# Row loads for the next sequence's statistics, asked for one unit earlier in the SP queue

## Chip, cores and metric

The kernel runs on one core of a Trainium2 chip. The metric is device time in microseconds (us) of one execution; the time of a kernel is the median of its timed runs. Beside them there is one execution under the hardware profiler, which has its own time and its own span (first to last instruction).

## What is computed

Routed attention over 4 sequences of 768 positions with 8 heads of 64, and then a block with layer norm and two weight matrices on the joined heads (512 wide, 2048 hidden):

```python
mask = q_assign[:, :, :, None] == k_assign[:, :, None, :]      # nearest of 16 centroids, q and k
scores = np.where(mask, scale * np.matmul(q, k.transpose(0, 1, 3, 2)), -1e9)
attn = softmax(scores)
x = np.matmul(attn, v)                                          # (B,H,S,D) -> (B,S,H*D)
...
mu = np.mean(x, axis=-1, keepdims=True)
var = np.mean((x - mu) ** 2, axis=-1, keepdims=True)
xn = (x - mu) / np.sqrt(var + 1e-06) * g_ln
ch = np.maximum(xn @ w_ch1, 0.0) @ w_ch2
return (x + ch).astype(np.float32)
```

The part that matters here is `mu` and `var` of each row of `x`, 768 rows for each sequence.

## The kernel before

**Stages.** The attention of all four sequences comes first (to about 318 us of the span). Its result `x` goes to DRAM twice: with the channels on the partitions (`xT_d`), and by rows (`x_d`: for each sequence six tiles of 128 rows by 512 columns). Then each sequence b = 0 to 3 passes the two weight layers: b = 0 from about 318 to 465 us, b = 1 to 603, b = 2 to 740, b = 3 to the end. While sequence b is in its first layer, the statistics of sequence b + 1 are made.

**Units.** The first layer of a sequence is cut into `NFH` = 8 units j = 0 to 7. For b = 1 a unit is `first_units(b, j)`: seven block products of a Strassen-Winograd scheme (`first_layer` with parts 1, 2, 4, 6, 3, 5, 7), each four matmul records of 128x384. A product goes to one of six PSUM banks (`ps_m`), and ScalarE (ACT) or VectorE (DVE) takes it out: `kept` (L878) is a copy by ACT, `add_relu` (L883) an addition by DVE, L891 the relu by ACT. For b = 2 a unit has smaller inner products besides (L1271); sequence 3 goes through `last_layer` and has no next sequence. The second layer of b = 1 to 3 is `deep_layer` (L1148).

**The statistics.** `rows_load(b, t)` (L557-561) asks for row tile t of sequence b: one DMA of 256 KB from `x_d[b][t]` into a buffer `xr`, of which there are two for b > 0. `norm_rows(b, t)` (L563-578) first calls `rows_load` for a later tile, and then, for b = 2 and 3, has ACT make the sum, the mean and the sum of squares of tile t (L572 to L574). So a buffer comes free when ACT has read the tile for the second time, at L574. `norm_stats`, at the end of unit 5, needs all six tiles.

Where the calls stand, for the tiles of sequence b + 1 in the first layer of b = 1 or 2:

- tiles 0 and 1 are asked for ahead of unit 0 (L1778-1779)
- tile 0 is worked on at the end of unit 0 (`unit_end(b, 0)`, L1740), and tile j in unit j = 1 to 5, after its product part 1 (L1628). At that point ACT stands between the copy `p` of part 1 (L878) and the relu of part 4 (L920)
- tile j + 1 is asked for by that same `norm_rows(b + 1, j)`, so it has the rest of unit j and the beginning of unit j + 1 to land

**The queues.** From the second sequence on (the block opened at L1731) the instructions of PE, DVE, ACT and SP stand in the order in which the Python code calls them. Nearly all DMAs of this stage are issued by SP, one after another; an issue that waits for a semaphore holds up those behind it.

**What else SP issues in b = 1.** `unit_end(1, j)` calls in this order: `leave(4)` (stores of turned rows, `x_d<-col`, L1221), `columns_load` (a load of 384 KB for the next turn, L534, for odd j), the four DVE operations of `w2_split` (L1065), pending jobs, ring loads for j > 4, the statistics' last steps, `leave` again, then `split()` (a store of 1 MB, `w_d<-wt`, L1066), and, for j = 1, 3, 4, `w2_back` (a load of 1 MB, `w_t`, L1044, which a split two units later reads).

**In b = 2** `unit_end` calls `leave(8)`: up to eight stores of finished output (`out_dram<-y`, L1221). `first_units` stores sums of w1 for the last sequence (L1311, L1320, L1322, L1330 into `w1_d`).

**The last sequence's loads.** `last_load(n, g)` (L1350-1359) brings such sums back. With n = 3 it issues two DMAs, into a buffer `a3` taken from the six of `unit` (192 KB) and into one of the two `xr` buffers (256 KB). The first of them, `last_load(3, 0)`, stands at L1784, right after the `deep_layer` of b = 2, which ends with products (3, 4) and (3, 3) and with `leave(len(leaving))` (L1596).

Of the kernel before, what the change touches and what calls it, by code (L numbers as in the profile page):

```python
# [23 lines left out]
def kernel(  # L24
# [12 lines left out]
    B, H, S, D = q.shape  # L37
# [519 lines left out]
    def rows_load(b, t):  # L557
        if t < NT and (b, t) not in rows:
            x = (ffn if b else last).tile([P, DM], F32, tag="xr", name="xr", bufs=2 + (not b))
            nc.sync.dma_start(out=x, in_=x_d[b][t])  # L560
            rows[b, t] = x

    def norm_rows(b, t):  # L563
        rows_load(b, t + 1 + (not b))
        x = rows.pop((b, t))
        if t == 0:
            moments[b] = small.tile([P, NT, 3], F32, tag="mv", name="mv")
        mv = moments[b]
        if b != 1:

            total, mean = mv[:, t, 0:1], mv[:, t, 1:2]
            nc.scalar.activation(x, x, AF.Identity, accum_out=total)  # L572
            nc.scalar.mul(mean, total, -1.0 / DM)
            nc.scalar.activation(x, x, AF.Square, bias=mean, accum_out=mv[:, t, 2:3])  # L574
            return
        bn = small.tile([P, 6], F32, tag="bn", name="bn")
        nc.vector.bn_stats(out=bn, in_=x)
        nc.vector.bn_aggr(out=mv[:, t, :2], in_=bn)
# [640 lines left out]
    def leave(n, queues=(nc.sync,)):  # L1219
        for i, (to, y) in enumerate(leaving[:n]):  # L1220
            queues[i % len(queues)].dma_start(out=to, in_=y)  # L1221
        del leaving[:n]
# [127 lines left out]
    def last_load(n, g):  # L1350
        if g >= NPU:
            return
        if n == 3:
            if "a3" not in last_w:
                last_w["a3"] = flat(unit("a3"))
            nc.sync.dma_start(out=last_w["a3"][:, : 3 * P], in_=w1_d[3][g][:, : 3 * P])
            nc.sync.dma_start(out=last_w[3], in_=w1_d[3][g][:, 3 * P :])
        else:
            nc.sync.dma_start(out=last_w[n][:, : w1_d[n].shape[2]], in_=w1_d[n][g])
# [102 lines left out]
    def deep_layer(b, more, st):  # L1462
# [64 lines left out]
        def onto(i, j):  # L1527
            return lambda: sum_onto(i, j)

        jobs = {  # L1530
            (4, 1): [lambda: first_layer(b, NFH - 1, 4) if more else outer_sums(NFH - 2, True)],
            (4, 2): [between],
            (4, 5): [lambda: rest_load(b, 0)],
            (4, 3): [rest(1, 0, 4)],
            (7, 6): [s4(0)], (7, 4): [s4(1)], (7, 3): [s4(2)], (1, 6): [s4(3)],
            (1, 4): [onto(4, 7)], (6, 3): [onto(6, 1)],
            (5, 4): [onto(4, 6)], (5, 3): [onto(5, 6)], (2, 6): [onto(7, 5)],
        }
# [3 lines left out]
        if more:  # L1542
            for at, (i, c) in (
                ((4, 4), (0, 0)), ((7, 5), (0, 1)), ((1, 3), (0, 2)), ((6, 6), (0, 3)),
                ((6, 5), (1, 0)), ((6, 4), (1, 1)), ((5, 6), (1, 2)), ((5, 5), (1, 3)),
            ):
                jobs.setdefault(at, []).append(norm(i, c))
            for at, c in (((4, 7), 1), ((7, 2), 2), ((7, 3), 3)):
                jobs.setdefault(at, []).append(lambda c=c: norm_load(b + 1, c))
            jobs[2, 4] = [out_of(1, 0, 4)]  # L1550
            jobs[2, 3] = [rest(0, 0, 2), lambda: rest_load(b, 1)]
            jobs[3, 6] = [lambda: x_sum(b + 1, 1), lambda: x_sum(b + 1, 2)]
            if b + 1 < LAST:
                jobs[3, 5] = [lambda: w1_sums(b + 1, 0, (0, 1))]
            else:
                jobs[2, 5].append(last_room)
                jobs.setdefault((2, 7), []).append(lambda: last_load(5, 0))
                jobs[2, 4].append(lambda: last_load(0, 0))
                jobs[3, 5] = [lambda: last_load(2, 0)]
            jobs[3, 7] = [lambda: first_layer(b + 1, 0, 1)]  # L1560
            later(
                *[None] * (b + 1 >= PAIRED), rest(1, 1, 7), out_of(1, 1, 7), out_of(0, 0, 2), None, *[None] * (b + 1 >= PAIRED),
                rest(0, 1, 3), out_of(0, 1, 3), None,
            )
        else:
            jobs[7, 2] = [lambda: rest_load(b, 1)]
            jobs[1, 3] = [rest(1, 1, 7)]
            jobs[5, 6] = [rest(0, 0, 1), onto(4, 6)]
            del jobs[5, 4]
            jobs[2, 5].append(rest(0, 1, 5))  # L1570
            jobs[2, 1] = [out_of(1, 0, 4)]
            jobs[2, 7].append(out_of(1, 1, 7))
            jobs[2, 3] = [out_of(0, 0, 2)]
# [91 lines left out]
    with tc.manual_schedule(engines={mybir.EngineType.PE, mybir.EngineType.DVE}):  # L1665
# [25 lines left out]
        def do(f, *args):  # L1691
# [4 lines left out]
        jobs = {  # L1696
            (1, 0): [
                do(first_layer, 0, NFH - 1, 4), do(first_layer, 0, NFH - 1, 3), do(relu, 1),
                do(hidden_sums, 1, range(3)),
            ],  # L1700
            (1, 1): [do(hidden_sums, 1, range(3, NFH - 1))],
            (1, 2): [do(hidden_sums, 1, range(NFH - 1, NFH)), do(w2_sum, st, 2), keep(2, 2)],
            (2, 0): [do(hidden_sums, 2, range(3))],
            (2, 1): [do(hidden_sums, 2, range(3, NFH))],
# [26 lines left out]
    with tc.manual_schedule(engines=order | {mybir.EngineType.SP}):  # L1731
        first.close()
        splits = first.enter_context(tc.tile_pool(name="splits", bufs=1))
        outer = {}

        def unit_end(b, j):

            if b + 1 < B:
                if j == 0:
                    norm_rows(b + 1, j)  # L1740
            if b == 1:
                leave(4)
                if asked and j % 2:
                    columns_load(row)
                if j == 0:
                    outer["ends"] = all_in_range()
                if j == 2:
                    outer["flag"] = flag_of(outer.pop("ends"))
                m = (1, 5, 3, 4, 2, 7, 6, None)[j]
                if m in SUMS:  # L1750
                    split = w2_split(m, outer.pop(("t", SUMS.index(m) + 1)))
                elif m:
                    split = w2_split(m, by_half(w2_block(*{1: (0, 0), 2: (1, 0), 3: (1, 1)}[m])))
                if j in (5, 6):
                    outer_late("s", "e", (0, 0), j - 5)
            while pending:
                job = pending.pop(0)
                if job is None:
                    break
                job()  # L1760
            if j > 4:
                for _ in range(4):
                    if ring["next"] < len(STEPS) * (b - 1) + RING:
                        ring_load(b)
            if b + 1 < B and j + 3 == NFH:
                norm_stats(b + 1)
            if b + 1 < B and j + 2 == NFH:
                norm_stat_rows(b + 1)
            leave(8 if b >= PAIRED else 4)
            if b == 1 and m:  # L1770
                split()
                if j in (1, 3, 4):
                    w2_back({1: 4, 3: 3, 4: 2}[j])

        for b in range(1, B):
            deep[b] = {}
            if b + 1 < B:
                rows_load(b + 1, 0)  # L1778
                rows_load(b + 1, 1)
            if b == 1:  # L1780
                w2_back(1)
                first_units(b, 0)
            elif b == LAST:
                last_load(3, 0)  # L1784
                last_layer(b)
            else:
                first_layer(b, 0, 6)
                w1_sums(b, 0, (2, 3))
                x_sum(b, 3)
                first_layer(b, 0, 5)  # L1790
                x_sum(b, 4)
                first_layer(b, 0, 7)
                w1_sums(b, 1)
                deep_room(b)
                outer_keep(b, 0)
                outer_keep(b, 1)
                pair_begin(b, 0)
            if b < LAST:
                unit_end(b, 0)
                for j in range(1, NFH):  # L1800
                    first_units(b, j)
                    unit_end(b, j)
                relu(len(summed))
            if b == LAST:
                pass
            elif b >= PAIRED:
                inner_sums(deep[b], ORDER[0], cs=slice(0, NQH - 1))
            else:
                inner_sums(deep[b], ORDER[0], cs=slice(NQH - 1, NQH))
            if b == 1:  # L1810
                first.close()
                units = pool("units", 1)
            deep_layer(b, b + 1 < B, deep[b])
        flag = outer["flag"]

# [230 lines left out]
```

## Time and profile before

| what | before |
|---|---|
| timed runs, us | 879.55, 880.76, 884.12 (median 880.76) |
| profiled execution, us | 884.5 |
| its span, us | 882.7 |
| busy in the span: PE, DVE, ACT | 98%, 83%, 46% |
| mean granted TensorE clock | 0.996 |
| first layer of b = 1, span us | 465 to 538 |
| first layer of b = 2, span us | 603 to 674 |

The page of a profile shows busy time by engine and by slice, the chain of work that ended last (followed back from the end), and groups of instructions with the idle time before them. PE is TensorE, PEld its weight loads, SPq SyncE issuing a DMA. A DMA issue is shown with the time at which it was issued; "us to landing" is the time from there until its data was there. The profiled execution is 3.7 us longer than the median of the timed runs; of that, 1.8 us lie outside its span.

### The profile page before, as it was taken

Reading aid. Unit: us, or ns where it says so; the run is one execution under the profiler, and the core shown is the slowest. Engines: PE = TensorE matmul, PEld = TensorE weight load, DVE = VectorE, ACT = ScalarE, POOL = GpSimd, SP = SyncE. Lnnn points to the kernel's source line nnn. Section 1 sums busy time; section 2 is a strip of 40 time slices with the busy share of each in tenths; the row PEclk is TensorE's granted clock in tenths of the full one; section 3 lists DMA queues with packets and bytes.
Section 4 is the critical chain, followed back from the end, with each engine's and each line's share of the span. In section 5 each row is a group of like instructions: output and inputs, shape, how many; then the busy total and the mean of one; then the engine's idle time right before and its main releaser. Section 6 shows DMA issues by size and latency. Waiting matters only on the chain.

```text
span 882.7 us, 13640 instructions
## 1 busy us (share of the span) xinstructions
PE 869.2 (98%) x4744; PEld 587.3 (67%) x4744; DVE 730.3 (83%) x1262; ACT 407.4 (46%) x758; POOL 77.6 (9%) x143
## 2 busy tenths in 40 slices
PE   8999999999999999999999899999999999999996
PEld 5444444444444445568886557997667998778996
DVE  6899999999999888959677677897877897767875
ACT  6777788888888823330004442102553111443110
POOL 1012121222222212110000000000000000000000
PEclk9999999999999999999999999999999999999999
DMA  7777889999986338876685789865567965564875
GB/s 160 138 128 128 150 172 189 194 217 190 185 193 181 98 108 210 235 193 218 182 196 165 228 257 307 275 193 144 130 185 247 294 202 148 128 185 124 275 196 112
DMA packets 258493, 164.68 MB, mean 187 GB/s; under 512 B 192992, under 2 KB 211440, under 8 KB 257392
## 3 DMA queue, kind: packets, MB, share of 16 engines
q1 hardware_dynamic: 227392, 144.43, 60.9%
q0 software_dynamic: 7776, 15.03, 8.8%
q10 hardware_dynamic: 23248, 4.25, 2.7%
q8 instruction: 40, 0.66, 0.3%
q14 instruction: 37, 0.30, 0.1%
HBM read 115.21 MB, written 40.07 MB: 176 GB/s over the span
## 4 chain that ended last, share of the span: by engine, by line
PE 93%; DMA 3%; DVE 1%; ACT 1%; SPq 1%; issue 0%; ACTq 0%; DVEq 0%
PE s_ps L401 17%; PE x_ps L852 17%; PE a_ps L413 14%; PE x_ps L1148 12%; PE z_ps L1148 6%; PE z_ps L852 6%; PE x_ps L961 5%; PE y_ps L1148 3%; PE z_ps L961 2%; PE x_ps L1271 2%; PE y_ps L852 2%; DMA xr<-x_d 2%; PE den_ps L469 1%; PE sim_ps L320 1%; PE y_ps L961 1%; PE z_ps L1271 1%
## 5 line engine op out<-in xcount | busy, mean ns | idle before, releaser
L401 PE MATMUL s_ps<-t,t 64*128 64x384 f32 x768 | 154.8, 483 | 0.0
L401 PEld LDWEIGHTS s_ps<-t,t 64*128 64x128 f32 x768 | 68.0, 187 | 39.0 <-issue 38.3
L1148 PE MATMUL x_ps<-lower,w 128*128 128x192 f32 x448 | 80.8, 326 | 0.5 <-DVE u L1163 0.5
L1148 PEld LDWEIGHTS x_ps<-lower,w 128*128 128x128 f32 x448 | 74.1, 190 | 1.6 <-DVE u L1163 0.7
L396 ACT ACTIVATE e<-s_ps 128x768 f32<-128x768 f32 x84 | 67.1, 812 | 6.9 <-PE s_ps L401 6.4
L396 ACT ACTIVATE w<-s_ps 128x768 f32<-128x768 f32 x80 | 64.5, 813 | 8.3 <-PE s_ps L401 7.7
L401 PE MATMUL s_ps<-mask,mask 64*128 64x384 bf16 x384 | 62.8, 323 | 1.0 <-ACT e L396 0.6
L891 ACT ACTIVATE lower<-lower 128x384 f32<-128x384 f32 x88 | 43.8, 520 | 42.2 <-DVE lower L883 28.7
L878 ACT COPY u<-x_ps 128x384 f32<-128x384 f32 x64 | 30.6, 478 | 62.1 <-PE x_ps L852 61.8
L413 PE MATMUL a_ps<-e,v_sb 128*64 128x384 f32 x336 | 57.6, 488 | 0.0
L878 ACT COPY p<-x_ps 128x384 f32<-128x384 f32 x32 | 15.3, 477 | 91.1 <-PE x_ps L852 85.9
L413 PE MATMUL a_ps<-w,v_sb 128*64 128x384 f32 x320 | 55.2, 488 | 0.0
L852 PE MATMUL x_ps<-xn,ws 128*128 128x384 f32 x128 | 48.1, 499 | 2.4 <-ACT u L878 2.4
L852 PE MATMUL x_ps<-xn,w 128*128 128x384 f32 x128 | 47.1, 491 | 0.0
L883 DVE TENSOR_TENSOR lower<-z_ps,u 128x384 f32<-128x384 f32 x40 | 22.2, 555 | 29.6 <-PE z_ps L852 20.3
L852 PE MATMUL x_ps<-xt,ws 128*128 128x384 f32 x128 | 46.6, 487 | 0.0
L852 PE MATMUL x_ps<-xt,w 128*128 128x384 f32 x128 | 46.5, 486 | 0.0
L413 PEld LDWEIGHTS a_ps<-e,v_sb 128*64 128x64 f32 x336 | 23.5, 137 | 31.8 <-issue 28.7
L1503 POOL DMA_DIRECT2D out_dram<-y_end x2 | 1.2, 598 | 487.2 <-DMA out_dram<-y 487.2
L413 PEld LDWEIGHTS a_ps<-w,v_sb 128*64 128x64 f32 x320 | 22.4, 137 | 30.4 <-issue 27.5
L401 PEld LDWEIGHTS <-mask 64*128 64x128 bf16 x384 | 19.0, 94 | 35.0 <-issue 10.0
L366 ACT ACTIVATE mask<-oh,far 32x384 bf16<-32x384 bf16 x61 | 37.3, 612 | 3.3 <-DVE oh L349 1.9
(296 smaller groups left out, 1807.8 us busy)
## 6 DMA issues: line engine op xcount, KB each, us to landing
w<-w_d SPq DMA_DIRECT2D x84, 256.0 KB, 3.2
raw<-in_moe_w_ch_dram SPq DMA_DIRECT2D x32, 512.0 KB, 4.9
w<-w_t SPq DMA_DIRECT2D x36, 256.0 KB, 4.6
w<-tb POOLq DMA_DIRECT2D x32, 256.0 KB, 5.6
w_d<-wt SPq DMA_DIRECT2D x7, 1024.0 KB, 5.4
w<-w_all SPq DMA_DIRECT2D x27, 256.0 KB, 3.1
v_sb<-in_v_dram SPq DMA_DIRECT2D x32, 192.0 KB, 4.5
xr<-x_d SPq DMA_DIRECT2D x24, 256.0 KB, 3.2
```

Source lines behind the costliest of these rows:

```text
L320: nc.tensor.matmul(sim[r : r + Q, :HC], cT[:, pr, :, :].rearrange("p j c -> p (j c)"), prepared[n][side][:, g * HC : (g + 1) * HC], start= ...
L366: nc.scalar.activation(out, oh[src, :], AF.Identity, bias=add, scale=factor)
L396: nc.scalar.activation(e, s[:, :, :HC], AF.Exp, scale=SCALE)
L401: nc.tensor.matmul(s[:, j, :HC], of_keys[:, keys], of_queries[:, o : o + HC], start=part == first, stop=part != first, skip_group_check=True,)
L413: nc.tensor.matmul(acc[j * D : (j + 1) * D, :HC], loaded[n]["v"][:, j, c, :], e[:, j, :], start=(c == 0), stop=(c == NT - 1),)
L852: nc.tensor.matmul(bank[:, :HC], lhs[:, c, :], rhs[:, c], start=first and c == 0, stop=c == NDH - 1, skip_group_check=True,)
L878: nc.scalar.copy(t, bank[:, :HC])
L883: nc.vector.tensor_tensor(h, bank[:, :HC], other, ALU.add)
L891: nc.scalar.activation(h, h, AF.Relu)
L961: nc.tensor.matmul(bank[:, :MH].rearrange("p (h f) -> p h f", h=2), hidden[lhs + (c,)][:, tt * P : (tt + 1) * P], rhs[:, :, c], start=firs ...
L1148: nc.tensor.matmul(bank, w[:, c, :], a[:, c], start=way in (1, 2, 5) and c == 0, stop=c == NQH - 1, skip_group_check=True,)
L1271: nc.tensor.matmul(bank, p["w"][way], p["x"][way], start=way in (1, 2, 5), stop=True, skip_group_check=True)
```

## The change

The load of row tile j + 2 is now called at the end of unit j (for j = 0 after `leave`, ahead of `split()`; for j > 0 at the very beginning of `unit_end`), for sequences 2 and 3. `norm_rows` asks for a later tile only for sequences 0 and 1, where the tile asked for is the same as before (t + 2 for 0, t + 1 for 1). `last_load(3, 0)` moves from the beginning of sequence 3 to a job after product (3, 4) of the `deep_layer` of b = 2. No arithmetic changes, and no buffer is added.

```diff
     def norm_rows(b, t):
-        rows_load(b, t + 1 + (not b))
+        if b < 2:
+            rows_load(b, t + 2 - b)
         x = rows.pop((b, t))
...
                 jobs[3, 5] = [lambda: last_load(2, 0)]
+                jobs.setdefault((3, 4), []).append(lambda: last_load(3, 0))
             jobs[3, 7] = [lambda: first_layer(b + 1, 0, 1)]
...
             if b + 1 < B:
                 if j == 0:
                     norm_rows(b + 1, j)
+                else:
+                    rows_load(b + 1, j + 2)
             if b == 1:
                 leave(4)
...
             leave(8 if b >= PAIRED else 4)
+            if j == 0 and b + 1 < B:
+                rows_load(b + 1, 2)
             if b == 1 and m:
                 split()
...
             elif b == LAST:
-                last_load(3, 0)
                 last_layer(b)
```

## The prediction, made before the changed kernel ran

> **What bounds the kernel now.** I read the page first (busy times, then the chain that ended last), then the chain in order of time for the first layer of b = 1, then the instructions of PE, ACT and SP there in order of time.
>
> ```profile
> PE   8999999999999999999999899999999999999996
> PE 93%; DMA 3%; DVE 1%; ACT 1%; SPq 1%; issue 0%; ACTq 0%; DVEq 0%
> ```
>
> PE is on the chain for 93% of the span and busy in nearly every slice. So a change of transfers can gain only where PE stands still; one slice in the middle is not full. The 3% of DMA on the chain are the place to look. In order of time:
>
> ```profile
> 478.26 5.05 DMA xr<-x_d
> ...
> 486.18 10.28 DMA xr<-x_d
> ...
> 499.08 0.38 ACT u L878
> 499.46 0.04 issue
> 499.50 4.54 PE x_ps L852 x8
> 504.04 1.29 PE y_ps L852 x4
> ```
>
> The columns are start, duration and what. Two row tiles of the next sequence are on the chain; the second takes 10.28 us to land and leads over ACT to a PE product. PE's own list around it:
>
> ```profile
> 494.36 1.45 PE L852 MATMUL z_ps<-xn,ws 128*128 128x384 f32 x4
> 495.65 1.45 PE L852 MATMUL z_ps<-xt,ws 128*128 128x384 f32 x4
> 499.50 2.80 PE L852 MATMUL x_ps<-xn,ws 128*128 128x384 f32 x4 [2.40 <-ACT u L878]
> 502.10 1.95 PE L852 MATMUL x_ps<-xn,w 128*128 128x384 f32 x4
> 503.88 1.45 PE L852 MATMUL y_ps<-xn,w 128*128 128x384 f32 x4
> ```
>
> One product starts 1.29 us after the one before it (495.65 - 494.36). Here the third starts 3.85 us after the second, and it and the next are slow besides. ACT, at the same time:
>
> ```profile
> 490.69 0.48 ACT L878 COPY p<-x_ps 128x384 f32<-128x384 f32 x1 [0.92 <-PE x_ps L852]
> 496.49 0.63 ACT L572 ACTIVATE xr<-xr 128x512 f32<-128x512 f32 x1 [5.32 <-DMA xr<-x_d]
> ```
>
> ACT waits 5.32 us for row tile 3 (unit 3), and the relus and bank copies queued behind it wait too. PE used up the free banks during the first 2.9 us of that and then stood. SP shows why the tile was late:
>
> ```profile
> 478.26 0.50 SPq L560 DMA_DIRECT2D xr<-x_d  x1
> 479.20 4.29 SPq L1221 DMA_DIRECT2D x_d<-col  x4
> 483.53 0.55 SPq L534 DMA_DIRECT2D col<-xT_d  x1
> 485.15 0.38 SPq L1066 DMA_DIRECT2D w_d<-wt  x1
> 485.58 0.51 SPq L1044 DMA_DIRECT2D w_t<-w_t  x1
> 486.18 0.38 SPq L560 DMA_DIRECT2D xr<-x_d  x1
> 493.28 0.37 SPq L1066 DMA_DIRECT2D w_d<-wt  x1
> 493.74 0.46 SPq L560 DMA_DIRECT2D xr<-x_d  x1
> ```
>
> The request stands behind the four small-grained stores, a load of 384 KB, a store of 1 MB and a load of 1 MB. From 483 to 492 us the view by stage gives a DMA share of 1.02 and 283 GB/s: the engines are full.
>
> **What the Trainium skill says.** "DMA: Bandwidth & Descriptors", section "Queues, rings and completion order", has the descriptors of one issuing engine consumed in ring order on the shared DMA engines. The trace agrees: 256 KB takes 10.28 us behind 2 MB, but 3.2 us in the median over all row tiles. Its "Rules for kernel authors" advise issuing a DMA early and waiting late, which is the form of this change. "TensorE: Matmul & The Clock Gate", section "What's actually happening", says that an idle PE falls to half clock and needs about 3.4 us of activity to return. The trace shows this, with a clock of 0.83 over 495 to 505 us and matmuls at twice their interval until about 503, but after an idle time of only 2.40 us (3.01 for weight loads), less than the page's window; the measurement counts.
>
> **The change, part by part.**
>
> Rows in b = 1. In the order of SP's instructions each request takes the place that the one before it had, and no other instruction changes its order:
> - tile 2 goes ahead of the split's first store. Its buffer is free once ACT has read tile 0 (473.23 + 0.19 = 473.4). SP has nothing between 467.4 and 477.8, so the wait for ACT holds up nobody. With the 5.0 us of the median landing in this stage it is there by 478.5; ACT wants it at 482.0. Its wait of 1.31 us goes.
> - tile 3 goes where tile 2 was, at 478.3. Its buffer is free at 475.5 (475.30 + 0.19). Landing took 5.05 us there, so 483.4; ACT wants it at 491.2. The wait of 5.32 us goes.
> - tile 4 takes the place at 486.2 and inherits the 10.28 us, so 496.5. ACT now wants it at 504.08 + 0.48 - 4.36 = 500.2 (4.36 is the gain worked out below): 3.7 us to spare.
> - tile 5 takes 493.74, where tile 4 landed before 504.4; it is wanted at 513.11 + 0.48 - 4.36 = 509.2, 4.8 us later.
>
> What PE gains: the third product due at 495.65 + 1.29 = 496.94 came at 499.50, 2.56 late. It took 2.60 to the next start in place of 1.29, 1.31 more, and that one 1.78, 0.49 more. Sum 2.56 + 1.31 + 0.49 = 4.36 us, all of it on the path, since PE is without a gap before and behind.
>
> What is moved past: the request of 256 KB now runs ahead of a split's store or of the four stores and the load of 384 KB. At 216 to 283 GB/s it is 0.9 to 1.2 us of DMA time and 0.4 to 0.5 us of SP. But the queue in front of each of them held the previous tile as well, so only the order within a unit shifts, by at most these 1.2 us. The reload of 1 MB (`w_t`, issued at 485.58, landing 8.0 us in the median and 8.7 at most) is read by DVE's split of unit 3, at 503.32 before and 499.0 now. It lands by about 494.3, or 495.5 with the shift: covered by 3.5 us. The stores of the split free a buffer two units later, and landed in 5.4 us. Cost 0.
>
> Rows in b = 2. Tile 2 keeps its place. Tiles 3, 4 and 5 go ahead of up to eight output stores, whose issue took 5.24 to 5.90 us. ACT's waits for them (2.19, 0.89 and 3.01 us) go. On PE only the last shows: 653.35 to 654.79 is 1.44, and 654.79 to 656.19 is 1.40, against 1.29 each, so 0.15 + 0.11 = 0.26 us. The stores come up to 1.2 us later; nothing but a later turn's buffer waits for them. Gain 0.26.
>
> `last_load(3, 0)`: its two DMAs stand in SP's order exactly where they stood, behind the last two stores (issued at 740.82 and 741.47), with no stores left after product (3, 4). PE first uses `a` at 752.81. Cost and gain 0; nothing in the trace waits for these two.
>
> Norm of sequences 0 and 1: the same tiles at the same places, 0.
>
> Sum: 4.36 + 0.26 = 4.62 us. In the profiled execution 884.5 becomes 879.9. I take the same gain from the median: 880.76 - 4.62 = 876.1 us.
>
> The doubtful term is how much of the 4.36 the timed runs have. The median lies 3.7 us below the profiled time, and the stall depends on a transfer's landing: if it came 2.9 us sooner (5.32 - 2.40), PE would not stop. So the lower bound of the term is 0, a loss by this term alone being excluded because no tile is asked for later. The upper bound: a landing 1.5 us worse adds 1.5. I take the full term, since the one execution that shows it is no outlier: 884.12 is among the timed runs.
>
> **The rivals.**
> - *The stall is largely the profiled execution's.* For: the 3.7 us above, and the half clock that comes only with a gap long enough. Against: the queue in front of tile 3 is the kernel's own, 2.7 MB at a full DMA share, and the timed runs have it too. It gives 0.3 to 1.5 us of gain: 879.5 to 880.5, say 880.0.
> - *Tile 4 takes over the wait.* It stands in the place that cost 10.28 us, with a margin of 3.7 us and then the 2.9 us that PE's banks cover. It would have to land 16.9 us after its issue to stop PE. Against: nothing is added to the queue. If half of the stall returned: 880.76 - 4.62 + 2.2 = 878.3.
> - *Slower: the requests hold up SP.* A request ahead of `leave` and of the split's store waits for ACT to free its buffer, and everything behind it on SP (stores, 384 KB, both transfers of 1 MB) waits along. Tile 5 is the tightest: ACT is done with tile 3 at about 493.4, and SP gets there at 493.7. Should the stores and reloads come so late that DVE's splits of units 3 and 5 wait for `w_t`, PE stops in both. That decides from a reload 4.7 us later than now, plus some 3 us of banks. Two stops of the size seen (4.36 each) against the gain: 880.76 + 8.7 - 4.6 = 884.9. Against: with the stall gone ACT is earlier, not later, and the margins above are all positive.
> - *A larger gain*: the timed runs have a longer stall, or the small gaps of b = 2 shrink too: 874.
>
> **How the numbers follow.** About 0.5% (4.4 us) is what a measurement of this kernel can tell from no change. My sum lies just above it. Forecast 0.66, of which 0.56 beyond the 0.5% and 0.10 below; stall of the profile 0.18; tile 4 0.05; slower 0.07; larger 0.04. Faster 0.56 + 0.04 = 0.60; same 0.10 + 0.18 + 0.05 = 0.33; slower 0.07. The range goes from 874.5 to 880.2: it leaves out the slower case, some of the larger gain and the end of the first rival.
>
> **What would show it.** Right: ACT has no wait for `xr` in units 2 to 5 of b = 1, PE has no gap near 497 and the clock of that stage is 1.00, so that the deep layer starts near 534.5 and not 538.8; tile 3 is issued near 478.3 and tile 4 near 486. In b = 2 the product after 653 keeps its 1.29 us. Wrong: ACT waits for tile 4 near 500; DVE waits for `w_t` in unit 3 or 5; SP waits for ACT at a row request with stores behind it; or the stage is shorter by 4 us and the median isn't, which is the first rival.

## The result, and the profile after

The changed kernel takes 879.50 us in the median of 22 runs (878.33 to 880.55), the kernel before 880.75 us in 22 runs beside them (878.73 to 884.12). The ratio is 0.9983, 95% interval 0.9975 to 0.9991: faster by 0.17%, 1.25 us. The forecast was 4.62 us.

The profile after, however, shows what was forecast. Its span is 877.7 us against 882.7, 5.0 us less. The slice of PE that was not full is full now (busy tenths in 40 slices, from the page of the changed kernel):

```profile
PE   8999999999999999999999999999999999999996
```

PE's list in order of time, at the place of the stall (changed kernel; start and duration in us):

```profile
494.33 1.45 PE L853 MATMUL z_ps<-xn,ws 128*128 128x384 f32 x4
495.62 1.45 PE L853 MATMUL z_ps<-xt,ws 128*128 128x384 f32 x4
496.91 1.45 PE L853 MATMUL x_ps<-xn,ws 128*128 128x384 f32 x4
498.20 1.45 PE L853 MATMUL x_ps<-xn,w 128*128 128x384 f32 x4
499.49 1.45 PE L853 MATMUL y_ps<-xn,w 128*128 128x384 f32 x4
```

Every product starts 1.29 us after the last. ACT, in the same view, takes up the row tiles of units 3 and 4 with no wait before them:

```profile
490.66 0.48 ACT L879 COPY p<-x_ps 128x384 f32<-128x384 f32 x1 [0.92 <-PE x_ps L853]
491.03 0.64 ACT L573 ACTIVATE xr<-xr 128x512 f32<-128x512 f32 x1
...
500.06 0.64 ACT L573 ACTIVATE xr<-xr 128x512 f32<-128x512 f32 x1
```

And SP's list has the requests where they were expected, each in the place of its predecessor:

```profile
473.41 0.32 SPq L560 DMA_DIRECT2D xr<-x_d  x1
477.80 0.37 SPq L1067 DMA_DIRECT2D w_d<-wt  x1
478.28 0.44 SPq L560 DMA_DIRECT2D xr<-x_d  x1
...
486.14 0.64 SPq L560 DMA_DIRECT2D xr<-x_d  x1
493.24 0.37 SPq L1067 DMA_DIRECT2D w_d<-wt  x1
493.70 1.80 SPq L560 DMA_DIRECT2D xr<-x_d  x1
```

So in these two profiled executions 5.0 us went, and in the median 1.25. Two theories could say why. **Theory 1**: the stall differs from one execution of the kernel before to the next, and the profiled one, at 884.5 us above all 22 timed runs, had one of the longest. **Theory 2**: the stall is always there, and the changed kernel gives some 3 us back at a place that its one profile doesn't show.

### The profile page after: what moved, and what is told of

Read it like the earlier page. It is cut to its first block, busy times and chain, and to the rows that moved or that the text cites. A ratio compares the mean times of both kernels' runs of the same rounds, so it can differ in the third digit from the quotient of the medians.

```text
span 877.7 us, 13639 instructions
## 1 busy us (share of the span) xinstructions
PE 866.4 (99%) x4744; PEld 586.6 (67%) x4744; DVE 730.3 (83%) x1262; ACT 409.1 (47%) x758; POOL 77.7 (9%) x143
## 4 chain that ended last, share of the span: by engine, by line
PE 95%; DMA 2%; DVE 1%; SPq 1%; ACTq 0%; ACT 0%; issue 0%; DVEq 0%
PE x_ps L853 19%; PE s_ps L401 17%; PE a_ps L413 14%; PE x_ps L1149 12%; PE z_ps L853 7%; PE z_ps L1149 6%; PE x_ps L962 5%; PE y_ps L1149 3%; PE z_ps L962 2%; PE y_ps L853 2%; PE x_ps L1272 2%; PE den_ps L469 1%; PE sim_ps L320 1%; PE y_ps L962 1%; PE z_ps L1272 1%; DMA out_dram<-y_end 1%
## 5 line engine op out<-in xcount | busy, mean ns | idle before, releaser
L1162 ACT COPY u<-x_ps 128x192 f32<-128x192 f32 x30 | 9.6, 319 | 63.6 <-PE x_ps L1149 59.1
```

The lines of the kernel that those rows point to most:

```text
L1162: nc.scalar.copy(o, rows_of(of))
```

## Experiments

Eight kernels, in two groups of four; the kernels of a group ran on one chip and share the runs of the kernel before (43 in the first group, 42 in the second).

**The kernel before once more.** No edit.

> The kernel before, unchanged, to see other executions of it. Theory 1 (the stall varies): the wait of ACT for row tile 3 in the first layer of b = 1 is usually shorter than the 5.32 us of the first profile, so PE stands for less than 2.4 us or not at all; this profile shows a PE gap of 0 to 1.5 us there, a span near 879, and the time equals before within 0.15%. Theory 2 (the stall is always there, and the changed kernel loses some 3 us elsewhere): this profile again shows a PE gap of about 2.4 us and half clock after it, span near 882.

Measured: 880.85 us, ratio 1.0000 (0.9989 to 1.0010). ACT and PE in order of time, in this other execution of the same program:

```profile
495.05 0.63 ACT L572 ACTIVATE xr<-xr 128x512 f32<-128x512 f32 x1 [3.58 <-DMA xr<-x_d]
```

```profile
495.95 1.45 PE L852 MATMUL z_ps<-xt,ws 128*128 128x384 f32 x4
498.06 1.56 PE L852 MATMUL x_ps<-xn,ws 128*128 128x384 f32 x4 [0.65 <-ACT u L878]
499.46 1.45 PE L852 MATMUL x_ps<-xn,w 128*128 128x384 f32 x4
500.75 1.45 PE L852 MATMUL y_ps<-xn,w 128*128 128x384 f32 x4
```

Row tile 3 landed 8.5 us after its request and not 10.28. ACT waits 3.58 us and not 5.32, PE stands 0.65 us and not 2.40, and no slow matmuls follow. From the second product's start to the start of the third after it are 4.80 us (500.75 - 495.95), against 3 x 1.29 = 3.87: PE loses 0.93 us, not 4.36. The span is 879.3 us. This is what theory 1 expected.

**Requests in b = 1 only.** As the change, but `norm_rows` still asks for a later tile for sequence 3, and the new calls are only made for b = 1:

```diff
-        rows_load(b, t + 1 + (not b))
+        if b != 2:
+            rows_load(b, t + 1 + (not b))
...
+                elif b == 1:
+                    rows_load(b + 1, j + 2)
...
+            if j == 0 and b == 1:
+                rows_load(b + 1, 2)
```

> Only the requests in the first layer of b = 1 (rows of sequence 2) are a unit sooner; those of b = 2 and the load of w1's sums stay as before. Theory 1: the whole gain of the change comes from here, 1.0 to 1.3 us, ratio about 0.9985. Theory 2: the stall of 4.4 us goes here and what is lost elsewhere stays away in part, so 2 to 4 us are gained.

Measured: 880.11 us, ratio 0.9988 (0.9980 to 0.9996), 0.8 us less than before. That fits theory 1 and lies below what theory 2 expected. PE has no gap near 497.

**Requests in b = 2 only.** The same with `b != 3`, `b == 2` and `b == 2`.

> Only the requests in the first layer of b = 2 (rows of sequence 3) are a unit sooner. Theory 1: 0 to 0.3 us gained, ratio 0.9997 to 1.0000. Theory 2, if the loss is made here by requests ahead of the output's stores: 1 to 3 us slower, ratio 1.001 to 1.0035.

Measured: 880.97 us, ratio 1.0003 (0.9995 to 1.0011). Nothing to be told from zero, and theory 2's loss isn't here. The profile shows both halves: ACT's three waits in b = 2 are gone, and in b = 1, which is here as in the kernel before, the stall is there once more, and short:

```profile
494.66 0.63 ACT L573 ACTIVATE xr<-xr 128x512 f32<-128x512 f32 x1 [3.49 <-DMA xr<-x_d]
```

```profile
495.66 1.45 PE L853 MATMUL z_ps<-xt,ws 128*128 128x384 f32 x4
497.67 1.56 PE L853 MATMUL x_ps<-xn,ws 128*128 128x384 f32 x4 [0.56 <-ACT u L879]
```

**The load of w1's sums only.** The two lines on `last_load(3, 0)` alone.

> Only the first load of w1's sums for the last sequence is called sooner. Theory 1: SP's order of requests is the same as before, so no difference, ratio 1.0000 within its interval. Theory 2, if the loss is made here: up to 3 us slower.

Measured: 880.84 us, ratio 0.9998 (0.9986 to 1.0009): no difference. A third short stall of the kernel before's form: ACT waits 4.12 us, PE stands 1.19 us.

With that, theory 2 has no place left: neither part loses anything, and four profiles of the b = 1 code of before give four stalls. What stayed open was whether the wait of this one tile is the whole gain, and how a wait becomes time.

**One tile, one place.** The kernel before, with row tile 3 asked for ahead of the reload of 1 MB and not behind it:

```diff
                 split()
+                if j == 1:
+                    rows_load(2, 3)
                 if j in (1, 3, 4):
                     w2_back({1: 4, 3: 3, 4: 2}[j])
```

> The kernel before with one request moved: row tile 3 is asked for right ahead of the 1 MB reload of w_t at the end of unit 1, in place of right behind it; all else as before. Cover theory (PE loses only what ACT's wait for tile 3 exceeds 2.9 us): the tile lands some 3.5 us sooner (1 MB at 283 GB/s), so ACT waits less than 1 us, PE has no gap, and the whole gain of the change in this stage is there: 0.8 to 1.4 us, ratio about 0.9988. If the gain needs all requests to be sooner (other tiles matter too): under 0.4 us.

Measured: 879.63 us, ratio 0.9980 (0.9974 to 0.9987). A single request moved past a single load brings 1.28 us, as much as the whole change brought. ACT's wait for the tile, in order of time:

```profile
491.47 0.63 ACT L572 ACTIVATE xr<-xr 128x512 f32<-128x512 f32 x1 [0.40 <-DMA xr<-x_d]
```

ACT still waits 0.40 us, and PE starts its products 1.29 us apart all through: a wait that the banks cover costs nothing.

**More in front of the tile.** The kernel before, with a store of two chunks of w2 (512 KB), or four (1 MB), to a place that nobody reads, ahead of the reload:

```diff
+    w2_x = spill.tile([P, 2, DM], F32, name="w2_x")          # 4 for 1 MB
...
                 split()
+                if j == 1:
+                    nc.sync.dma_start(out=w2_x, in_=w2[:, :2, :])
                 if j in (1, 3, 4):
```

> The kernel before with a store of 512 KB more (two chunks of w2 to an unused place) at the end of unit 1, ahead of the w_t reload and so of row tile 3. Cover theory: tile 3 lands 1.8 us later (512 KB at 283 GB/s), ACT waits 5.3 to 5.9 us, PE's gap is 2.4 to 3 us, half clock for some 4 us follows as in the first profile, and the median goes up by 3 to 4 us (ratio 1.0035 to 1.0045). If the first profile's half clock was an accident apart from the gap, 1.8 us (1.002).

> The same with a store of 1 MB more. Cover theory: tile 3 lands 3.7 us later, ACT waits 7.2 to 7.8 us, PE's gap is 4.3 to 4.9 us with half clock after it, 5 to 5.7 us slower than before (ratio 1.0057 to 1.0065). If PE's banks do not cover a fixed 2.9 us, another gap.

Measured: 884.26 us with 512 KB, ratio 1.0032 (1.0019 to 1.0046); 885.21 us with 1 MB, ratio 1.0049 (1.0036 to 1.0061). With 512 KB, PE's list and the view by stage (columns of the latter: PE, weight loads, DVE, ACT, POOL busy, then granted clock, DMA share, GB/s):

```profile
495.72 1.45 PE L852 MATMUL z_ps<-xt,ws 128*128 128x384 f32 x4
500.07 2.93 PE L852 MATMUL x_ps<-xn,ws 128*128 128x384 f32 x4 [2.90 <-ACT u L878]
502.79 1.69 PE L852 MATMUL x_ps<-xn,w 128*128 128x384 f32 x4
504.31 1.45 PE L852 MATMUL y_ps<-xn,w 128*128 128x384 f32 x4
```

```profile
495.00:505.00 10.00, 7.11 (x18) 3.79 (x17) 4.53 (x10) 4.69 (x13) 0.00 (x0) 0.83 0.76 203
```

This is the picture of the first profile again, brought about by an edit: a gap of 2.90 us, a clock of 0.83 over these 10 us, a product of twice its length behind it. PE loses 504.31 - 495.72 - 3.87 = 4.72 us; with 1 MB the same sum gives 5.39. The eight timed runs with 512 KB are not all of this kind: three of them take 882.2 to 882.8 us at a mean clock of 0.998 or 0.999, the other five 883.7 to 885.7 at 0.996 or 0.997. So here too one profile is one draw, and the median stands for a mixture. The expectation for 1 MB had the size of ACT's wait too high (7.2 to 7.8 us; 6.36 came), and so the ratio: the tile landed 2.8 us later on the clock than in the unchanged kernel's second profile (497.8 against 495.0), where 3.7 were expected.

**The change with more in front.** The changed kernel with the same store of 1 MB, which there stands ahead of row tile 4:

> The changed kernel with the same store of 1 MB more at the same place, ahead of row tile 4 there. Cover theory: tile 4 lands near 500 where ACT wants it at 500.1, so at most 1 us of ACT's wait, no PE gap, and the time stays that of the changed kernel, ratio to before 0.998 to 0.9995. If the transferred bytes themselves cost time, 3.7 us slower than the changed kernel, ratio about 1.0025.

Measured: 879.42 us, ratio 0.9983 (0.9977 to 0.9990), the changed kernel's own time. The added MB cost 4.3 us in the kernel before and nothing here. In this profile one row tile took 11.4 us to land, the longest of all, and ACT waited for none. So here the bytes and the queue as such cost nothing that can be measured; only a tile that comes too late does.

## Why the prediction was wrong

**The step that failed** is the one named the doubtful term: how much of the 4.36 us the timed runs have. The text took it in full "since the one execution that shows it is no outlier: 884.12 is among the timed runs". It was one. Its 884.5 us exceed every one of the 22 runs of the kernel before that stood beside the changed one, of which two came near it (883.98 and 884.12). How rare such an execution is, the runs of the experiments show, since each has the mean clock of the whole execution on record. That is 0.996 in the three profiles in which the clock fell, and 0.997 to 0.999 in the other seven. Of the 125 runs of kernels with the b = 1 code of before, six have 0.996; they take 883.3 to 885.3 us, and all others at most 882.8. Of the 74 runs of kernels in which tile 3 comes sooner, none has it. By this sign about one execution in twenty has the long stall that was priced for all.

The bound on this term had an error besides. It says that PE would not stop if the tile came 2.9 us sooner, "(5.32 - 2.40)". But 2.9 us is the part of the wait that the banks cover; the gap is the other part, so 2.40 us sooner is enough. With that the stall looked harder to lose than it was.

Row tile 3 landed after 10.28 us there, after 8.5, 8.5 and 9.1 us in the other three profiles with the b = 1 code of before. The ten profiles give one table of how that wait becomes time (the lost time is taken from PE's starts, as above):

| profile | ACT's wait for tile 3, us | PE's gap, us | PE's lost time, us |
|---|---|---|---|
| tile 3 ahead of the reload | 0.40 | 0 | 0 |
| requests in b = 2 only | 3.49 | 0.56 | 0.83 |
| before, second profile | 3.58 | 0.65 | 0.93 |
| sums' load only | 4.12 | 1.19 | 1.46 |
| before, first profile | 5.32 | 2.40 | 4.36 |
| 512 KB more | 5.82 | 2.90 | 4.72 |
| 1 MB more | 6.36 | 3.43 | 5.39 |
| changed; changed with 1 MB; requests in b = 1 only | 0 | 0 | 0 |

The gap is the wait less 2.92 to 2.93 us in every row where there is one. The lost time is the gap and 0.27 us up to a gap of 1.19, and the gap and 1.8 to 2.0 us from 2.40 on, where the clock falls (the last section has its length). So a landing only 1.2 us later (9.1 to 10.28) triples the loss (1.46 to 4.36), and the first profile lay on the far side of that step. The usual loss, the mean of the three short ones, is 1.07 us. That agrees with the 1.25 measured, whose interval goes from 0.8 to 2.2 us; the 0.26 of b = 2, which the run with that part alone doesn't show, would make it 1.33. The lengthened kernels agree as well: 4.72 - 1.07 = 3.65 against 3.35 measured, where the median stands for a mixture, and 5.39 - 1.07 = 4.32 against 4.30. That 879.50 lies inside the stated range of 874.5 to 880.2 doesn't speak for the sum: the upper end was set to take in most of the first rival.

**Right**: the place, the cause and the mechanism. Tile 3 was late behind the store and the reload; ACT held the banks; PE stopped when the cover was used up, and the 2.9 us of cover read off one execution held in five more. In the changed kernel's profile ACT waits for no row tile in this stage. The rows of b = 2 lost their waits on ACT, with an effect on PE too small to measure here. The sums' load did nothing.

**The rivals.** "The stall is largely the profiled execution's" was the right one in its kind, at 880.0 us, half a microsecond above what came; its reason, that profiling makes it, isn't shown, since executions near 884 stand among the timed runs as well. Tile 4 did stand in the late place and, with 1 MB more in front of it, waited for nothing. SP's wait for ACT, the rival on the slower side, is 6.0 us long ahead of the request at 473.41, where nothing was queued behind it. The rival's tightest place, tile 5 at 493.70, did hold up SP: that request occupied it for 1.80 us, and the four stores behind it went out at 495.60 in place of 494.63. PE had no gap from it.

**Open**: why the same tile behind the same queue lands after 8.5 us in one execution and 10.3 in another. The DMA share from 483 to 492 us is full in all four profiles (1.02 to 1.04). The reload right in front of the tile landed after 8.7 us in the first profile and after 8.4 to 9.0 in the others. But the tile followed the reload by 2.2 us in the first, and by 0.6 to 0.7 in the others. So the difference arose after the reload had landed and not in the queue up to it; its cause isn't shown. The remaining part of the 5.0 us between the two first profiles beyond 4.62, some 0.4 us, is open too.

## What to carry to other kernels

A stall behind a full DMA queue is a distribution, and one profile is one draw from it. If the profiled execution lies above the timed runs, first subtract: here its excess over the median (3.7 us) is time that the median doesn't have, and a gap whose length depends on a landing is the first suspect. Where a wait is covered up to some length and a long gap also costs clock, take the cover from the trace and price the usual wait; and look for the one request that matters, as moving it past one load may be the whole gain.

## What the runs showed of the hardware that was not expected

PE's clock fell to half after a gap of 2.40 us (3.01 us without weight loads), and again after 2.90 and 3.43; after 1.19 us it did not. The first profile, in windows of 1 us (columns as above; the third number from the end is the clock):

```profile
499.00:500.00 1.00, 0.50 (x1) 0.38 (x2) 0.00 (x0) 1.00 (x4) 0.00 (x0) 0.83 0.86 135
500.00:501.00 1.00, 1.00 (x3) 0.52 (x2) 0.65 (x2) 0.28 (x1) 0.00 (x0) 0.50 1.11 148
501.00:502.00 1.00, 1.00 (x3) 0.48 (x2) 0.46 (x1) 0.00 (x0) 0.00 (x0) 0.50 0.68 155
502.00:503.00 1.00, 1.00 (x3) 0.60 (x2) 0.15 (x1) 0.48 (x1) 0.00 (x0) 0.50 0.49 197
503.00:504.00 1.00, 1.00 (x4) 0.57 (x4) 1.00 (x2) 0.00 (x0) 0.00 (x0) 0.96 0.00 0
```

Worked out from such windows, the half clock lasts 3.4 us in each of the three profiles. At half speed that is 1.7 us, and the fall did cost 1.55 to 1.69 us beyond the 0.27 us by which a short gap's restart is slower. By the same estimate it begins some 0.2 us after PE's restart here, 0.9 us after it with 1 MB more, and 0.2 us before it with 512 KB. So the length of the gap alone doesn't set its moment. The Trainium skill, "TensorE: Matmul & The Clock Gate", section "What's actually happening", puts the idle window at about 3.4 us; in two of these three profiles a shorter gap was enough.

The same request can occupy SP for very different times: 1.80 us at 493.70 in the changed kernel, 0.46 us at 493.74 in the kernel before. The fill of the DMA engines doesn't explain it, since their share from 493 to 496 us is 0.69 and 0.74. The view of SP's waits puts 1.8 us of it down to ACT, but ACT had done with the tile that sat in this buffer at 492.85 (492.66 + 0.19). What held it is open.
